# Gated linear attention and channel MLP on one core: keys and queries in three blocks of 384 columns, a new load order at the start, and a re-planned feed-forward

## The chip, the cores and the metric

The kernel runs on one core of one Trainium2 chip. The time is device microseconds of one launch; most executions of one kernel agree within 0.3%. The median of three runs of the kernel before is 1095.43 us (1094.91 to 1096.3).

## The reference

With x of 2048 tokens by 576 channels, all float32:

```python
g = sigmoid((x * gate_w).sum(-1, keepdims=True))
# a: linear attention, 32 heads of 18, phi(t) = where(t > 0, t + 1, exp(t)) + 1e-6
q, k, v = heads(x @ wqkv)                       # wqkv: 576 x 1728
kv, z = einsum("sd,se->de", phi(k), v), phi(k).sum(0)      # per head
o = (phi(q) @ kv) / (phi(q) @ z + 1e-6)
a = o @ wo
# b: mixer channel MLP
h = gelu(layernorm(x) @ w1 + b1)                # w1: 576 x 4608
b = h @ w2 + b2                                 # w2: 4608 x 576
out = g * a + (1 - g) * b
```

## The kernel before

**Precision.** TensorE multiplies in fp32r. Each operand is split into a high part and a low remainder, ScalarE (ACT) rounding the high part and VectorE (DVE) subtracting. A product of a tile of x (576 rows: four chunks of 128 and a tail of 64) with a block of weights is 14 matmuls: `HH`, `HL`, `LH` and two for the tail. `BY_ROWS` and `HI_FIRST` are two orders of those 14.

**Stage 1, keys and queries.** x is cut into 16 tiles of 128 tokens, taken in the order `ORDER`. For each tile `project(i, part, half)` makes the keys and the queries in two halves of 288 columns each, four blocks of 14 matmuls into PSUM banks 6 and 7 in turn. The second half of the keys carries two more columns, the gate's sum and the row sum (290 columns). `phi` then needs two ACT instructions (Relu, Exp) and one DVE instruction a half. `keys_split` splits the keys, and `add_products` (19 matmuls in two parts of 8 and 11) adds the tile's product of keys and x into banks that stay for the whole stage. The queries of a tile go to `acc[i]`.

**The start.** The first three tiles (`FIRST = 3`) are written out by hand. SyncE (SP) issues the loads in the order of the program: x of the first tile, x of the second, the second half of the key weights, x of the third, the first half of the query weights, and so on; ACT's queue loads the first half of the key weights in pieces. The weights are split on ACT and DVE (`split_w`) in the order in which they stand. `first_keys(n, half)` and `first_queries(n, half)` are the 14 matmuls of tile n. The gate's column is transposed in through `turn_gate`.

**The loop** over tiles 3 to 15 (`for n in range(FIRST, NT)`) does per tile: keys half 0, keys half 1, first part of `add_products` of the tile before, queries (both halves), second part. Jobs of the normalized rows (`Y_JOBS`) are hung into numbered slots. The last three tiles (`LATE = 3`) leave their queries for later: one set after the loop, one before the key-value products, one between `transpose_q(0)` and `transpose_q(1)`.

**Stage 2, values.** `project_values(t)` multiplies the masked key-value matrix with the output weights into a pair of banks (`w_pairs`: 6 and 4 in turn), then ACT copies the high part and DVE subtracts the low one into `wp`. `normalize(i, parts)` divides the queries of a tile by their denominators on DVE, and `tail_q(i)` copies the tail on ACT. The order of these calls by hand is the order on each engine.

**Stage 3, attention.** `attend(i)` multiplies 16 tiles of queries with `wp`, 28 matmuls each.

**Stage 4, feed-forward.** Two superblocks of 1024 tokens times 18 chunks of 256 hidden columns. An "up" product (7 a chunk, by a Strassen-like scheme `FACTORS`) is 7 matmuls of 512 columns in two parts of 4 and 3; a "down" unit is 6 (or 12) matmuls of 288 columns. Sums of weights and of hidden parts are put on DVE or on GpSimd (POOL) by the set `ON_DVE`. Chunks in `FIVES` fold their partial sums with copies on ACT in the place of some of the additions on DVE (`make_units`). `plan` simulates all engines with costs (`COST`, and `HEAR`, the time for which a finished instruction is not yet known to the next engine), due times from `TUNED`, and picks the order of all instructions. On TensorE it does a down unit as soon as its slot has come and its inputs are ready within 100 ns, otherwise an up part; `late` says how many parts the ups may run ahead of a down that is not ready. The order that comes out is the order in which each engine runs.

Of the kernel before, what the change touches and what calls it, by code (L numbers as in the profile page):

```python
# [9 lines left out]
F32 = mybir.dt.float32  # L10
F32R = mybir.dt.float32r
AF = mybir.ActivationFunctionType
# [26 lines left out]
LATE = 3  # L39
# [45 lines left out]
DVE_SUMS = set([(2, False), (2, True), (3, True), (4, False), (4, True), (6, False), (6, True)])  # L85
SEEDS = ((0, 0, 0), (0, 1, 1), (1, 0, 1))
Y_EARLY = 5000
ON_DVE = set([('h', 0, 2), ('h', 0, 6), ('h', 1, 3), ('h', 2, 2), ('h', 2, 6), ('h', 3, 4), ('h', 3, 6), ('h', 4, 2), ('h', 5, 3), ('h', 5, 6), ('h', 6, 2), ('h', 6, 3), ('h', 6, 6), ('h', 7, 2), ('h', 7, 6), ('h', 8, 4), ('h', 8, 6), ('h', 9, 4), ('h', 9, 6), ('h', 10, 2), ('h', 10, 4), ('h', 11, 2), ('h', 11, 6), ('h', 12, 4), ('h', 12, 6), ('h', 13, 4), ('h', 14, 4), ('h', 14, 6), ('h', 15, 2), ('h', 15, 4), ('h', 16, 6), ('h', 17, 3), ('h', 17, 4), ('w1', 2, 0), ('w1', 3, 0), ('w1', 10, 0), ('w1', 12, 0), ('w1', 14, 0), ('w1', 16, 0), ('w1', 17, 0), ('w2', 0, 0), ('w2', 4, 0), ('w2', 5, 0), ('w2', 8, 0), ('w2', 10, 0), ('w2', 11, 0), ('w2', 12, 0), ('w2', 14, 0), ('w2', 16, 0)])
FIVES = set([1, 2, 3, 4, 5, 7, 8, 9, 10, 11, 12, 14, 15, 16])
TUNED = (6, 7, 0, 1000, 0, {'unit': -1500, 'ytl': 1500, 'h': -1500, 'yst': 700, 'yhi': -300, 'y': -1500, 'w2': -3000, 'sum': 700, 'p': 700, 'ylo': 300, 'w1sum': -700, 'w1raw': 1500, 'evict': -1500, 'w2hi': -700, 'fin': -700, 'q2': -1500, 'seed': -3000, 'hi': -3000, 'ynorm': 3000, 'forked': -1500, 'ysum': -1500, 'q4': 6000, 'whole': 700, 'u3': -700, 'b2b': -3000, 'q1': 10000, 'out': -300, 'u1': -300, 'end': -700, 'q3': 700, 'w1st': 3000, 'attn': -700, 'fold': -300, 'w2raw': 300, 'yraw': 700}, [2, 5, 250, -500, 600, {'sum': 700, 'u3': 700, 'end': -1500, 'w2sum': -700, 'out': -3000, 'unit': -1500, 'p': -700, 'h': -300, 'evict': -700, 'hi': -1500, 'w1sum': 10000, 'seed': 3000, 'forked': 3000, 'y': 3000, 'q2': -3000, 'u1': -1500, 'q4': 6000, 'w1st': 300, 'ysum': 300, 'w2': 300, 'yraw': 1500, 'whole': 300, 'ynorm': 10000, 'attn': -3000, 'ytl': -1500, 'w1raw': -300, 'q1': 1500, 'yst': 300, 'fin': -300, 'yhi': 700, 'w2raw': 1500, 'w1': 300, 'w2hi': 6000, 'fold': 10000, 'b2b': 700}])  # L90
# [36 lines left out]
def tile_gated_mix(ctx: ExitStack, tc: tile.TileContext, x, xm, xe, wm, we, wvm, wve, wo, um, ue, w2, b1, b2, gw, out):  # L127
# [71 lines left out]
    W, at_ = {}, 0  # L199
    for part in (KEY, QUERY):  # L200
        for half in range(2):
            n = HALF + 2 * (part == KEY and half)
            W[part, half] = ym[:, at_:at_ + 10 * n].rearrange("p (a n) -> p a n", n=n)
            at_ += 10 * n
# [42 lines left out]
    def split_x(i, pieces=((0, 5),)):  # L247
        if i not in xs:
            xs[i] = x_places[PLACE[i] % X_RING]
        to, src = xs[i], xraw[i]  # L250
        for t0, t1 in pieces:
            act.activation(to[:, t0:t1], src[:, t0:t1], AF.Copy)
# [16 lines left out]
    def project(i, part, half, order=BY_ROWS, n=None, between={}):  # L269
        w = W[part, half]  # L270
        p = banks[i, part, half] = ps[:, next(halves_in) if n is None else n]
# [5 lines left out]
    def projected(i, part):  # L277
        for half in range(2):
            project(i, part, half)

    def phi(dst, i, part, half, also=lambda: None):

        p, own = banks[i, part, half][:, :HALF], half_cols(half)
        e = tmp.tile([P, HALF], F32, name="e")
        act.activation(e, p, AF.Relu, scale=-1.0)
        act.activation(e, e, AF.Exp, scale=-1.0)
        also()
        dve.scalar_tensor_tensor(dst[:, own], p, 0.0, e, op0=OP.max, op1=OP.add)
# [3 lines left out]
    def keys_phi(i, half):  # L292
        if half == 0:
            K[i] = kp.tile([P, D], F32, name="k")
        phi(K[i], i, KEY, half, (lambda: None, lambda: sums_of_x(i))[half])

    def sums_of_x(i):
        own = slice(PLACE[i], PLACE[i] + 1)
        act.activation(gsum[:, own], banks[i, KEY, 1][:, HALF:HALF + 1], AF.Copy)
        act.activation(nmean[:, own], banks[i, KEY, 1][:, HALF + 1:HALF + 2], AF.Copy, scale=-1 / D)  # L300
# [21 lines left out]
    def queries_out(i):  # L322
        for half in range(2):
            phi(acc[i], i, QUERY, half)
# [135 lines left out]
    load_x(first[1])  # L460
    load_w(KEY, 1)
    load_x(first[2])
# [10 lines left out]
    split_x(first[0], ((0, 4),))  # L473
# [4 lines left out]
    def first_keys(n, half, between={}):  # L478
        project(first[n], KEY, half, HI_FIRST, 3 * half + n, between)

    def first_queries(n, half):
        project(first[n], QUERY, half, HI_FIRST)

    def both_phi(n):
        for half in range(2):
            keys_phi(first[n], half)
# [32 lines left out]
    phi(acc[first[0]], first[0], QUERY, 0)  # L519
# [4 lines left out]
    phi(acc[first[1]], first[1], QUERY, 0)  # L524
# [3 lines left out]
    phi(acc[first[2]], first[2], QUERY, 0)  # L528
# [6 lines left out]
    phi(acc[first[0]], first[0], QUERY, 1)  # L535
    add_products(first[1], 0)
    phi(acc[first[1]], first[1], QUERY, 1)
# [5 lines left out]
    phi(acc[first[2]], first[2], QUERY, 1)  # L543
# [80 lines left out]
    wo_parts = [ym[:GW, a * G * D:(a + 1) * G * D].rearrange("p (j n) -> p j n", j=G) for a in range(2)]  # L624
    kv_parts = [x_places[PLACE[late[0]] % X_RING - 1][:GW], y_place[:GW, :len(PIECES) * P].rearrange("p (t n) -> p t n", n=P)]
# [21 lines left out]
    projected(late[0], QUERY)  # L647
# [62 lines left out]
    project(late[1], QUERY, 0, n=4)  # L710
    project(late[1], QUERY, 1, n=0)
# [63 lines left out]
    project_values(2)  # L775
    normalize(1, (1,))
    tail_q(1)
    project_values(3)
    project_values(4)
# [3 lines left out]
    for half in range(2):  # L783
        project(late[2], QUERY, half, n=4 + half)
    transpose_q(1)
    tail_q(2)
    queries_out(late[2])
    a1.close()
# [121 lines left out]
    HEAR = {PE: 155, ACT: 33, DVE: 33, POOL: 78, DMA: 30}  # L910
# [140 lines left out]
    def sum_on(what, k, m=0):  # L1051
        own = ((what, k, m) in ON_DVE) != ((m, k < NCHUNK) in DVE_SUMS)
        return (DVE, dve) if own else (POOL, pool)
# [25 lines left out]
    def make_w1(k):  # L1079
# [5 lines left out]
        if k > 1:  # L1085
            dma(lambda: load_w1(k), raw_free["w1"] if k > 2 else [], [("w1raw", k)], 4400, 8, each=560)
            for n in range(4):
                engine, eng = sum_on("w1", k)
# [33 lines left out]
    def make_w2(k):  # L1122
# [4 lines left out]
        if seven:  # L1127
            for n in range(4):
                engine, eng = sum_on("w2", k)
                op(engine, lambda n=n, eng=eng: sum_w2(n, eng), HALF, needs=[("w2raw", k)] + ([("w2sum", k, n - 1)] if n else []),  # L1130
                   gives=[("w2sum", k, n)], port=True)
# [315 lines left out]
    def plan(lag, late, slop, slack, guard, ahead, second=None):  # L1447
        second = second or (lag, late, slop, slack, guard, ahead)
# [23 lines left out]
        next_up, next_down, shift = 0, 0, 0.0  # L1472
# [35 lines left out]
        def choose(e, gently):  # L1508
            if e == PE:
# [4 lines left out]
                if a and b:  # L1514
# [5 lines left out]
                    if ta is not None and tb is not None:  # L1520
                        if tb <= ta + 100:
# [22 lines left out]
        while any(pending.values()):  # L1544
# [6 lines left out]
            e, t = o.engine, s + o.tail  # L1551
            if e == PE:
                shift = s - nominal[o]
                if o.by[0] == "up":
                    next_up += 1
                    if next_up == SECOND:
                        late, slop, slack, guard = second[1:5]
                else:
# [21 lines left out]
            else:  # L1580
                free[e] = s + o.ns
# [62 lines left out]
```

## Time and profile before

| | |
|---|---|
| median of three runs | 1095.43 us |
| the profiled execution | 1096.17 us, its span 1094.5 us |
| TensorE (PE) busy | 1086.3 us, 6712 matmuls |
| DVE, ACT, POOL busy | 922.4, 691.3, 236.2 us |
| granted TensorE clock | 1.00 |
| keys and queries, start to the first kv product | to about 187 us |
| values | 192 to 206 us |
| attention | 206 to 273 us |
| feed-forward | 273 us to the end |

Times of single instructions count from the start of the span. A matmul's row in the profile lasts longer than its turn, since matmuls overlap: a group's pace is read from the start of one group to the start of the next. The name after the engine is the tile written, then those read: `y` holds the weights and x in the first stage and the normalized rows in the feed-forward, `s` is a freshly loaded weight, `t` a freshly loaded x, `region` the split w2, `wa` and `wb` the split w1.

### The profile page before, as it was taken

What the parts mean: (1) busy time and instruction counts of PE and PEld (TensorE: products, weight loads), DVE (VectorE), ACT (ScalarE), POOL (GpSimd) and SP (SyncE); (2) the same over time, 40 slices, a digit from 0 to 9 for tenths busy, and PEclk for the clock granted to TensorE, in tenths of its full rate; (3) what the DMA queues carried; (4) which work ended last, traced back from release to release, by engine and by line L of the source; (5) the groups of instructions that cost most, each with busy time, mean ns of one, the idle gap of its engine ahead of it and who ended that gap; (6) DMA issues with size and microseconds to landing.
All of it is one profiled execution on the core that took longest, in us unless ns stands there. A gap on an engine that the chain in (4) does not pass through costs nothing.

```text
span 1094.5 us, 18650 instructions
## 1 busy us (share of the span) xinstructions
PE 1086.3 (99%) x6712; PEld 996.6 (91%) x6712; DVE 922.4 (84%) x1558; ACT 691.3 (63%) x1235; POOL 236.2 (22%) x232
## 2 busy tenths in 40 slices
PE   9999999999999999999999999999999999999998
PEld 8999999999898889988889988989899999999898
DVE  4568786896799999899999997988887888878888
ACT  6677766454667887777877876455555555455552
POOL 2111113431123232332111202121122211221110
PEclk9999999999999999999999999999999999999999
DMA  6466772745745665764556559574444445444432
GB/s 179 135 87 190 172 218 101 278 178 191 249 156 188 196 203 185 239 209 169 194 184 220 191 197 396 170 252 118 135 148 118 130 119 148 131 122 118 133 102 87
DMA packets 109006, 189.72 MB, mean 173 GB/s; under 512 B 8940, under 2 KB 68604, under 8 KB 104818
## 3 DMA queue, kind: packets, MB, share of 16 engines
q1 hardware_dynamic: 108002, 187.78, 53.7%
q8 instruction: 53, 0.87, 0.3%
q10 hardware_dynamic: 720, 0.74, 0.2%
q14 instruction: 39, 0.32, 0.1%
q0 software_dynamic: 192, 0.01, 0.0%
HBM read 121.70 MB, written 66.80 MB: 172 GB/s over the span
## 4 chain that ended last, share of the span: by engine, by line
PE 92%; DVE 3%; DMA 3%; ACT 1%; issue 0%; SPq 0%; ACTq 0%; DVEq 0%
PE ps L120 92%; DVE accs L120 1%; DMA accs<-moments 1%; DMA yd<-ystage 1%; DMA s<-in_wm 0%; DVE h L120 0%; DMA ystage<-late_acc 0%; DMA fresh<-in_ue 0%; DMA s<-in_we 0%; DVE wa L120 0%; DVE region L120 0%; DVE ystage L120 0%; DVE wb L120 0%; DVE fresh L120 0%; ACT u L120 0%
## 5 line engine op out<-in xcount | busy, mean ns | idle before, releaser
L120 PEld LDWEIGHTS ps<-region,h 128*128 128x128 f32 x3072 | 437.5, 188 | 30.2 <-ACT ps L120 4.7
L120 PE MATMUL ps<-region,h 128*128 128x288 f32 x3072 | 456.8, 295 | 0.8 <-DVE accs L120 0.7
L120 DVE TENSOR_TENSOR accs<-ps,accs 128x576 f32<-128x576 f32 x330 | 246.1, 753 | 60.7 <-PE ps L120 53.9
L120 PE MATMUL ps<-y,wa 128*128 128x512 f32 x1008 | 257.6, 392 | 0.0
L120 PEld LDWEIGHTS ps<-y,wa 128*128 128x128 f32 x1008 | 180.8, 188 | 30.5 <-ACT ps L120 0.2
L120 POOL TENSOR_TENSOR fresh<-fresh 128x288 f32<-128x288 f32 (+1 forms) x128 | 117.1, 918 | 409.5 <-DVE accs L120 144.5
L120 PE MATMUL ps<-y,wb 128*128 128x512 f32 x756 | 199.2, 393 | 0.4 <-ACT u L120 0.4
L120 DVE TENSOR_TENSOR h<-u,h 128x512 fp32r<-128x512 f32 x240 | 165.4, 702 | 8.7 <-ACT u L120 8.7
L120 PEld LDWEIGHTS ps<-y,wb 128*128 128x128 f32 x756 | 133.8, 188 | 21.1 <-ACT u L120 0.6
L120 PE MATMUL ps<-y 128*128 128x288 f32 (+2 forms) x950 | 133.9, 297 | 2.2 <-DVE wp L120 1.1
L120 PEld LDWEIGHTS ps<-y 128*128 128x128 f32 (+1 forms) x950 | 129.8, 188 | 4.4 <-DVE wp L120 1.8
L120 ACT ACTIVATE region<-fresh 128x576 fp32r<-128x576 f32 (+1 forms) x132 | 81.2, 625 | 73.9 <-PE ps L120 73.3
L120 ACT ACTIVATE ps<-ps 128x576 f32<-128x576 f32 (+1 forms) x127 | 78.6, 621 | 45.0 <-PE ps L120 21.5
L120 POOL TENSOR_TENSOR u<-u 128x512 f32<-128x512 f32 x44 | 57.1, 1298 | 193.2 <-DVE h L120 54.8
L120 DVE TENSOR_TENSOR region<-fresh,region 128x576 fp32r<-128x576 f32 (+1 forms) x132 | 94.3, 727 | 1.1 <-ACT region L120 1.1
L120 ACT ACTIVATE u<-ps 128x512 f32<-128x512 f32 x73 | 43.0, 589 | 68.2 <-PE ps L120 68.2
L120 ACT ACTIVATE h<-u 128x512 fp32r<-128x512 f32 x128 | 73.4, 621 | 9.9 <-DVE u L120 5.5
L120 ACT ACTIVATE h<-u,b1s 128x512 fp32r<-128x512 f32 x73 | 52.6, 722 | 42.2 <-DVE u L120 42.1
L120 PE MATMUL ps<-wp,qt 128*128 128x288 f32 x448 | 63.0, 297 | 0.0
L120 DVE TENSOR_TENSOR u<-ps,u 128x512 f32<-128x512 f32 x74 | 50.4, 683 | 13.6 <-PE ps L120 12.7
L120 PEld LDWEIGHTS ps<-wp,qt 128*128 128x128 f32 x448 | 59.8, 188 | 0.0
L120 DVE TENSOR_TENSOR u<-u 128x512 f32<-128x512 f32 x84 | 58.0, 691 | 1.7 <-POOL u L120 1.1
(139 smaller groups left out, 1044.8 us busy)
## 6 DMA issues: line engine op xcount, KB each, us to landing
w1d<-wa SPq DMA_DIRECT2D x17, 1280.0 KB
wa<-w1d SPq DMA_DIRECT2D x68, 320.0 KB
fresh<-in_w SPq DMA_DIRECT2D x70, 288.0 KB
y<-yd SPq DMA_DIRECT2D x14, 1280.0 KB
w1d<-wb SPq DMA_DIRECT2D x17, 960.0 KB
wb<-w1d SPq DMA_DIRECT2D x51, 320.0 KB
yd<-ystage SPq DMA_DIRECT2D x28, 320.0 KB
fresh<-in_um SPq DMA_DIRECT2D x64, 128.0 KB
```

The costliest lines, as they stand in the source:

```text
L120: self.last = self.tc.keep_in_program_order(op(*args, **kwargs))
```

## The change

Three things are edited.

1. **Blocks of 384.** From the fourth tile on, the keys and queries of a tile are three blocks instead of four halves: block 0 is keys 0 to 383; block 1 is keys 384 to 575, the two sum columns and queries 0 to 191 (386 columns); block 2 is queries 192 to 575. The split weights lie in one array so that the blocks are slices of it; the first three tiles still use the halves. `LATE` becomes 4, and only block 2 is left for later. The places of two later operands (`wo_parts`, `kv_parts`) follow the new layout.
2. **The start and the hand-written order.** The third x is loaded ahead of the second half of the key weights, and split and multiplied with the first half before that second half is split. The high part of the first x is copied on DVE and not on ACT. The first half of the query weights is split ahead of `both_phi(0)`. In stage 2 `project_values(3)` moves ahead of `normalize(1, (1,))`, and `tail_q(1)` behind `project_values(4)`.
3. **The feed-forward's plan.** `HEAR` becomes 65 ns for ACT and DVE (33 before), 110 for POOL (78), 300 for DMA (30). TensorE's runs are costed by the place of a matmul in its run (`EACH`). The sets `ON_DVE` (each sum for itself) and `FIVES` (13 chunks, 14 before: 3 and 16 leave, 17 comes) and the numbers of `TUNED` are new; a rule `hold` and `wait` is added.

```diff
-LATE = 3
+LATE = 4
+BLOCK = 384
+REST = D - BLOCK
...
-FIVES = set([1, 2, 3, 4, 5, 7, 8, 9, 10, 11, 12, 14, 15, 16])
-TUNED = (6, 7, 0, 1000, 0, {...}, [2, 5, 250, -500, 600, {...}])
+HEAR_NS = {"PE": 155, "ACT": 65, "DVE": 65, "POOL": 110, "DMA": 300}
+FIVES = set([1, 2, 4, 5, 7, 8, 9, 10, 11, 12, 14, 15, 17])
+TUNED = (6, 12, 0, 0, -500, {...}, [2, 5, 250, -1000, 2000, {...}, 21, 0], 7, 0)
...
+    at_ = 10 * (2 * D + 2)
+    weights = ym[:, :at_].rearrange("p (a n) -> p a n", a=10)
+    FIRST_Q = D + 2
+    W = {(KEY, 0): (0, HALF), (KEY, 1): (HALF, FIRST_Q), (QUERY, 0): (FIRST_Q, FIRST_Q + HALF), (QUERY, 1): (FIRST_Q + HALF, FIRST_Q + D),
+         0: (0, BLOCK), 1: (BLOCK, FIRST_Q + REST), 2: (FIRST_Q + REST, FIRST_Q + D)}
...
+    def keys_phi(i, n):
+        if n in (0, (KEY, 0)):
+            K[i] = kp.tile([P, D], F32, name="k")
+        if n == 0:
+            phi(i, n, [(K[i][:, :BLOCK], 0)])
+        elif n == 1:
+            phi(i, n, [(K[i][:, BLOCK:], 0), (acc[i][:, :REST], REST + 2)], lambda: sums_of_x(i, n, REST))
+        else:
+            phi(i, n, [(K[i][:, half_cols(n[1])], 0)], lambda: sums_of_x(i, n, HALF) if n[1] else None)
...
     load_x(first[1])
+    load_x(first[2])
     load_w(KEY, 1)
-    load_x(first[2])
...
-    split_x(first[0], ((0, 4),))
+    split_x(first[0], ((0, 4),), on_dve=True)
...
     first_keys(1, 0)
+    split_x(first[2])
+    first_keys(2, 0)
     dve.tensor_copy(wraw[KEY, 1][:, :, HALF:HALF + 1], column[:, :, None])
     dve.memset(wraw[KEY, 1][:, :, HALF + 1:HALF + 2], 1.0)
     split_w(KEY, 1)
-    split_x(first[2])
     load_x(ORDER[3])
     first_keys(0, 1)
     first_keys(1, 1)
+    split_w(QUERY, 0)
     both_phi(0)
-    split_w(QUERY, 0)
-    first_keys(2, 0)
     first_keys(2, 1)
...
-        project(i, KEY, 0)
+        project(i, 0)
         keys_phi(i, 0)
-        project(i, KEY, 1)
+        project(i, 1)
...
         if n < NT - LATE:
-            projected(i, QUERY)
+            project(i, 2)
             queries_out(i)
...
     project_values(2)
+    project_values(3)
     normalize(1, (1,))
+    project_values(4)
     tail_q(1)
-    project_values(3)
-    project_values(4)
     normalize(2, (0,))
     transpose_q(0)
     normalize(2, (1,))
-    for half in range(2):
-        project(late[2], QUERY, half, n=4 + half)
+    for n in range(2):
+        project(late[2 + n], 2, at_=4 + n)
...
-    HEAR = {PE: 155, ACT: 33, DVE: 33, POOL: 78, DMA: 30}
+    HEAR = HEAR_NS
+    EACH = {"up": (226.8, (6.3, 9.3, -2.7, 4.3, 9.3, 1.5, 5.5, 4.2)), "down": (131.9, (0, 3, -1, -2, 7, 1, 2, 3, -6, 1, 0, 1))}
...
-                        if tb <= ta + 100:
+                        if tb <= ta + 100 and not (run[0] == "up" and run[1] < hold and behind < wait and ta <= free[PE]):
                             ta = None
```

More of the change, by code (lines that the diff above doesn't have):

```diff
@@ L198, in tile_gated_mix @@
     TERMS = ((0, 0), (0, 1), (1, 0))
-    W, at_ = {}, 0
-    for part in (KEY, QUERY):
-        for half in range(2):
-            n = HALF + 2 * (part == KEY and half)
-            W[part, half] = ym[:, at_:at_ + 10 * n].rearrange("p (a n) -> p a n", n=n)
-            at_ += 10 * n
+    at_ = 10 * (2 * D + 2)
[3 more added lines that the diff above has]
+         0: (0, BLOCK), 1: (BLOCK, FIRST_Q + REST), 2: (FIRST_Q + REST, FIRST_Q + D)}
+    W = {key: weights[:, :, c0:c1] for key, (c0, c1) in W.items()}
     y_place = ym[:, at_ + X_RING * 9 * P:][:, :2 * 5 * P]
@@ L267, in tile_gated_mix, with project @@
     halves_in, banks = cycle((6, 7)), {}
-    def project(i, part, half, order=BY_ROWS, n=None, between={}):
-        w = W[part, half]
-        p = banks[i, part, half] = ps[:, next(halves_in) if n is None else n]
+    def project(i, n, order=BY_ROWS, at_=None, between={}):
+        w = W[n]
+        p = banks[i, n] = ps[:, next(halves_in) if at_ is None else at_]
         for m, (a, b) in enumerate(order):
@@ L322, in queries_out, with half_queries_out @@
     def queries_out(i):
-        for half in range(2):
-            phi(acc[i], i, QUERY, half)
+        phi(i, 2, [(acc[i][:, REST:], 0)])
+    def half_queries_out(i, half):
+        phi(i, (QUERY, half), [(acc[i][:, half_cols(half)], 0)])
     KC = 448
@@ L518, in tile_gated_mix @@
     both_phi(2)
-    phi(acc[first[0]], first[0], QUERY, 0)
+    half_queries_out(first[0], 0)
     split_xn(first[0])
@@ L523, in tile_gated_mix @@
     first_queries(2, 0)
-    phi(acc[first[1]], first[1], QUERY, 0)
+    half_queries_out(first[1], 0)
     for part in range(2):
@@ L527, in tile_gated_mix @@
     split_w(QUERY, 1)
-    phi(acc[first[2]], first[2], QUERY, 0)
+    half_queries_out(first[2], 0)
     first_queries(0, 1)
@@ L542, in tile_gated_mix @@
     add_products(first[1], 1)
-    phi(acc[first[2]], first[2], QUERY, 1)
+    half_queries_out(first[2], 1)
     keys_split(first[2])
@@ L646, in tile_gated_mix @@
     split_wo(2, 4)
-    projected(late[0], QUERY)
+    project(late[0], 2)
     queries_out(late[0])
@@ L787, in tile_gated_mix @@
     queries_out(late[2])
+    queries_out(late[3])
     a1.close()
@@ L1445, in tile_gated_mix, with plan @@
     assert len(in_order) == len(ops)
-    def plan(lag, late, slop, slack, guard, ahead, second=None):
-        second = second or (lag, late, slop, slack, guard, ahead)
+    def plan(lag, late, slop, slack, guard, ahead, second, hold, wait):
         slot, due = {o: n for n, o in enumerate(ups)}, {}
@@ L1471, in plan, with streams @@
         port_at, moved, landed = {e: 0 for e in port_until}, 0.0, []
-        next_up, next_down, shift = 0, 0, 0.0
+        next_up, next_down, shift, run = 0, 0, 0.0, ["", 0]
+        def streams(o):
+            n = round(o.ns / (231.7 if o.by[0] == "up" else 132.3))
+            each, more = EACH[o.by[0]]
+            at_ = run[1] if run[0] == o.by[0] else 0
+            return n, n * each + sum(more[at_:at_ + n])
         def offer(o):
@@ L1550, in plan @@
             s, _, o = min(picks, key=lambda x: x[:2])
-            e, t = o.engine, s + o.tail
+            e, t, ns = o.engine, s + o.tail, o.ns
             if e == PE:
+                n, ns = streams(o)
+                t += ns - o.ns
+                run[:] = o.by[0], n + (run[1] if run[0] == o.by[0] else 0)
                 shift = s - nominal[o]
@@ L1557, in plan @@
                         late, slop, slack, guard = second[1:5]
+                        hold, wait = second[6:8]
                 else:
```

63 lines of the change are left out of this document (30 added, 33 removed).

## The prediction

> **What bounds the kernel now.** I read the page first, then the list of waits of TensorE, then busy time by stage, then the timeline where something waits.
>
> ```profile
> span 1094.5 us, 18650 instructions
> PE 1086.3 (99%) x6712; PEld 996.6 (91%) x6712; DVE 922.4 (84%) x1558; ACT 691.3 (63%) x1235; POOL 236.2 (22%) x232
> PE 92%; DVE 3%; DMA 3%; ACT 1%; issue 0%; SPq 0%; ACTq 0%; DVEq 0%
> ```
>
> The second line is the busy time of each engine, the third the chain of work that ended last. TensorE (PE) is the bound. Its waits, and the stages (columns: stretch, its length, busy time and count of PE, weight loads, DVE, ACT, POOL, granted clock, DMA share, GB/s):
>
> ```profile
> PE ps L120 <- DVE wp L120: 1.1, 1, 1.1
> ...
> PE ps L120 <- DVE accs L120: 0.7, 1, 0.7
> PE ps L120 <- ACT u L120: 0.4, 1, 0.4
> ```
>
> ```profile
> 14.48:192.00 177.52, 177.52 (x1194) 170.06 (x1194) 124.65 (x267) 125.21 (x280) 32.45 (x25) 1.00 0.56 148
> 273.10:700.00 426.90, 426.40 (x2502) 381.79 (x2501) 398.27 (x657) 319.45 (x528) 103.21 (x98) 1.00 0.61 209
> 700.00:1090.50 390.50, 389.81 (x2338) 353.90 (x2336) 329.82 (x498) 202.87 (x334) 72.33 (x76) 1.00 0.45 134
> ```
>
> The reader should see that PE is full for the whole key and query stage, at clock 1.00, and that there are few waits to take away. So the time can fall in two ways only: fewer or shorter matmuls, or those few waits. Every part is costed as PE time.
>
> **Part 1, blocks of 384.** Per tile 56 matmuls of 288 (half of the keys 290) become 42 of 384 to 386; the columns stay the same, so what is saved is the part of a matmul that doesn't depend on its columns. One period of the loop, PE alone:
>
> ```profile
> 78.64 3.88 PE L120 MATMUL ps<-y 128*128 128x288 f32 x28
> ...
> 84.34 3.90 PE L120 MATMUL ps<-y 128*128 128x288 f32 x28
> 88.08 0.85 PE L120 MATMUL ps<-xs,ks 128*128 128x512 f32 x3
> 88.77 1.23 PE L120 MATMUL ps<-ks,xs 128*128 128x512 f32 x5
> 89.84 3.88 PE L120 MATMUL ps<-y 128*128 128x288 f32 x28
> ```
>
> Start to start, 28 matmuls of 288 take 88.08 - 84.34 = 3.74 us, 133.6 ns each; three of 512 take 88.77 - 88.08 = 0.69 us, 230 ns each. A line through both is 0.430 ns a column and 9.7 ns fixed; at 384 it gives 174.9 ns. A tile then takes 42 x 174.9 = 7.35 us in the place of 7.48, a gain of 0.13 us. The 0.69 is rounded; with 0.68 (227 ns) the line gives 173.6 ns and 0.19 us. I take 0.15 us, 13 tiles: **-2.0 us** (1.7 to 2.5). It doesn't matter where in the stage a block runs, since PE is full there, so `LATE = 4` costs nothing as long as no bank is waited for: blocks alternate between two banks and each has 14 matmuls of another block, some 2.4 us, to be emptied by two ACT instructions and one DVE pass, which is longer than now (1.87 us). ACT issues six instructions of `phi` a tile and not eight; DVE keeps four. ACT has 125 of 178 us, so this moves nothing.
>
> [...]
>
> **Part 2, the start.** The second half of the key weights is waited for:
>
> ```profile
> 4.69 0.74 SPq L120 DMA_DIRECT2D s<-in_wm  x1
> ...
> 7.90 0.58 SPq L120 DMA_DIRECT2D t<-in_xm  x1
> ...
> 8.56 3.45 PE L120 MATMUL ps<-y 128*128 128x288 f32 x24
> ...
> 11.30 1.42 ACT L120 ACTIVATE y<-s 128x1450 fp32r<-128x1450 f32 x1 [2.43 <-DMA s<-in_we]
> ...
> 12.75 1.67 DVE L120 TENSOR_TENSOR y<-s,y 128x1450 fp32r<-128x1450 f32 x1 [2.80 <-ACT y L120]
> 12.77 1.48 PE L120 MATMUL ps<-y 128*128 128x290 f32 x9 [0.76 <-ACT y L120]
> ...
> 14.48 12.14 PE L120 MATMUL ps<-y 128*128 128x290 f32 x89 [0.23 <-DVE y L120]
> ```
>
> ```profile
> 4.70:11.20 6.50, 6.50 (x44) 6.14 (x44) 3.77 (x10) 3.15 (x7) 0.00 (x0) 1.00 0.90 250
> ```
>
> PE ends the first-half products of two tiles at 8.56 + 24 x 0.134 = 11.77. It starts on the second half at 12.77, does the nine matmuls that need only high weights by 13.97, and waits for DVE's low part until 14.48: 1.0 + 0.5 us lost. After the change 14 more matmuls stand in that hole, to 13.64. Their price is on the queue: on SP the third x (two more loads behind it) takes the places from 4.69 on, and the weights move to 7.90. The DMA engines were 0.90 busy at 250 GB/s, so the delay is the bytes of one x, 5 x 128 x 128 x 4 = 328 KB: 1.3 us. The weights land at 12.6, ACT splits to 14.02, PE starts at 14.05, its nine end at 15.25, DVE's low part is there at 15.7, and the 33 left end at 20.15. Before, the same work (47 matmuls after 14.48) ended at 20.78: **-0.6 us**. Bounds: without any delay of the weights all 42 run from 13.64 to 19.27, -1.5; with the full 7.90 - 4.69 = 3.2 us they end at 22.0, +1.3. I take the bytes, since the engines were nearly full.
>
> What else moves here I cost at nothing. The third x is split on ACT and DVE between 9 and 11.3, when ACT waits (the 2.43 in its row). The copy of the first x on DVE takes 128x512 off ACT, but PE's first products wait for pieces of weights that still come when they came. `split_w(QUERY, 0)` now stands on ACT before the first `phi`, which waits for PE anyway; were those weights late, `phi` would queue behind, and with it the banks of the first keys, which `add_products` needs only after the first queries.
>
> **Part 3, the values.** The longest wait of PE (1.1):
>
> ```profile
> 198.68 1.26 DVE L120 SCALAR_TENSOR_TENSOR accs<-accs,den 128x576 f32<-128x576 f32 x1
> ...
> 199.82 0.60 PE L120 MATMUL ps<-accs 128*128 128x128 f32 x4
> 199.98 0.31 ACT L120 ACTIVATE tail<-accs 128x128 f32<-128x128 f32 x1 [2.00 <-DVE accs L120]
> 200.19 1.17 ACT L120 ACTIVATE wp<-ps 128x576 fp32r<-128x576 f32 x2
> ...
> 200.86 1.42 DVE L120 TENSOR_TENSOR wp<-ps,wp 128x576 fp32r<-128x576 f32 x2 [0.92 <-ACT wp L120]
> 201.67 3.99 PE L120 MATMUL ps<-y 128*128 128x288 f32 x28 [1.14 <-DVE wp L120]
> ```
>
> The late queries use the banks of `project_values(3)`. Its ACT copy stands behind `tail_q(1)`, which waits (2.00) for the normalization on DVE (198.68 to 199.94). After the change the copy follows its matmuls, whose last six (of `project_values(4)`) end at 199.8, so it can start by 199.0: ACT to 199.65, DVE to 200.35. PE ends its transposes at 200.5 and goes on. **-1.1 us** (0 to 1.14). Late next: the normalization, now 200.35 to 201.6, then the `wp` of the last piece to 202.3 and tile 2's first part to 203.6; they are needed by the attention, which starts two blocks (4.9 us) later, at 206. `tail_q(1)` has the same room.
>
> **Part 4, the feed-forward.** No matmul is added or removed. What can go is waits and the price of changing between ups (512) and downs (288):
>
> ```profile
> 714.11 0.86 PE L120 MATMUL ps<-y,wb 128*128 128x512 f32 x3
> 715.65 1.59 PE L120 MATMUL ps<-region,h 128*128 128x288 f32 x10 [0.69 <-DVE accs L120]
> ```
>
> ```profile
> 279.51 4.92 PE L120 MATMUL ps<-y,wb 128*128 128x512 f32 x21
> 284.27 6.56 PE L120 MATMUL ps<-y,wa 128*128 128x512 f32 x28
> ...
> 400.69 1.78 PE L120 MATMUL ps<-y,wa 128*128 128x512 f32 x7
> 402.31 1.75 PE L120 MATMUL ps<-region,h 128*128 128x288 f32 x12
> ```
>
> At 714 three ups take 1.54 us where 0.69 is due: 0.85 us lost, more than the 0.69 that the row shows as idle; the other wait is 0.4. In a long run an up takes (284.27 - 279.51)/21 = 226.7 ns, in a run of seven (402.31 - 400.69)/7 = 231.4. The new plan knows this price, but its rule `hold` acts only where `behind < wait`, with `wait` 0, while a down is not considered at all where `behind` is below 0: it is inert, and runs stay near seven. So I take the two waits: **-1.2 us**. Best: those and a quarter of 1764 x 4.7 ns = 8.3 us, -3.3. Worst by DVE, whose work grows in the first superblock:
>
> ```profile
> L120 DVE TENSOR_TENSOR accs<-ps,accs 128x576 f32<-128x576 f32 x330 | 246.1, 753 | 60.7 <-PE ps L120 53.9
> L120 DVE TENSOR_TENSOR u<-u 128x512 f32<-128x512 f32 x84 | 58.0, 691 | 1.7 <-POOL u L120 1.1
> L120 DVE TENSOR_TENSOR fresh<-fresh 128x384 f32<-128x384 f32 x28 | 15.4, 572 | 0.5 <-DMA fresh<-in_ue 0.5
> ```
>
> One chunk of `FIVES` fewer is four more additions of 753 ns; counting the sets, five more sums of 572 ns and two fewer of 691 come to DVE there: 3.0 + 2.9 - 1.4 = +4.5 us, on 398 of 427 busy. It hides in the 29 us left; without that cover it costs up to 4.5.
>
> **The sum.** -2.0 - 0.6 - 1.1 - 1.2 = -4.9 us. Against the profiled execution's 1096.17 that is 1091.3; the median of the runs is 0.7 lower, so **1090.5**.
>
> **The rivals.**
> (a) *The plan changes nothing*: inert rule, other small waits for the old. For it: only two waits to win in 817 us of feed-forward. 1095.4 - 3.7 = 1091.7.
> (b) *A matmul's time is all columns*: 384/288 x 133.6 = 178.1 ns, 42 of them 7.48 us, part 1 gains nothing: 1092.5. Against it: 512 columns by this would take 237.5, and take 230. [...]
> (c) *The feed-forward gives it back*: new waits of 3 to 4 us (DVE is at 93% in the first superblock), total 1094 to 1096. For it: 0.85 us went at a single place in the present order. Within 0.2%.
> (d) *Slower*: DVE becomes the bound of the first superblock. The added 4.5 us land on PE, and each down that waits for its addition also stops the ups behind it; at one wait like 714's (0.85 us) in six of the 18 chunks, 5.1 more: 1095.4 - 3.7 + 9.6 = 1101.3. It decides when more than 3.7 us land on PE, measurably at 5.9. Against it: 29 us of idle DVE.
>
> **How the numbers follow.** 0.2%, 2.2 us, is about what a measurement of this kernel can tell from no change. Forecast 0.56, (a) 0.13, (b) 0.05, (c) 0.18, (d) 0.08. Forecast, (a) and (b) are faster: 0.74; (c) same, 0.18; (d) slower, 0.08. Low end: all best bounds, 1.5 + 2.5 + 1.14 + 3.3 = 8.4, to 1087.0. High end 1094.6, into (c): it leaves out (d) and a good half of (c).
>
> **What would show it.** The loop's period 11.20 (78.64 to 89.84) falls to 11.05; PE has 13 x 14 = 182 fewer matmuls, 6530; the wait for `wp` is gone; the split of the 1450-column weights starts near 12.6 and the first-stage waits there sum to 0.9; the first up starts 3.7 us earlier, at 269.4; DVE's busy time to 700 rises by about 4 us without a wait of PE over 0.5. Wrong if the period stays at 11.2, or the feed-forward from its first up to the end is not between 818 and 822 us (now 821.4).

## The result and the profile after

The changed kernel takes 1101.52 us (median of 5 runs, 1100.64 to 1102.66), the kernel before in the same session 1095.8: a ratio of 1.0057, 95% interval 1.0047 to 1.0068. It is slower by 0.57%, where 0.4% faster was forecast. The profiled execution is the slowest of the five, 1102.66 us. The page of after, the lines that answer to those of before:

```profile
span 1101.0 us, 18199 instructions
PE 1086.8 (99%) x6530; PEld 999.2 (91%) x6530; DVE 932.4 (85%) x1583; ACT 687.8 (62%) x1202; POOL 219.0 (20%) x212
```

PE has the 182 matmuls fewer, and yet is as long busy as before: a row's busy time hides a part of what a matmul waits for (0.16 of the 0.85 us lost at 714.11 in the profile of before) and what a slower clock adds (in a stretch at clock 0.50, below, 3.41 of 3.41 us are busy). What PE waits for (total, times, longest):

```profile
PE ps L122 <- ACT y L122: 5.1, 5, 2.0
PE ps L122 <- DVE accs L122: 2.3, 1, 2.3
PE ps L122 <- DVE y L122: 1.8, 3, 1.1
...
PE ps L122 <- DVE wp L122: 0.2, 1, 0.2
```

The wait for `wp` is down to 0.2, as forecast, and the waits for `y` and `accs` are 9.2 us in the place of 1.7. Four starts on PE cut each span into pieces, those of before first (start, length, work), then those of after:

```profile
39.54 3.63 PE L120 MATMUL ps<-y 128*128 128x288 f32 x26
...
181.44 1.13 PE L120 MATMUL ps<-pks,ones 128*128 128x288 f32 x4
...
273.13 6.54 PE L120 MATMUL ps<-y,wa 128*128 128x512 f32 x28
```

```profile
8.89 5.29 PE L122 MATMUL ps<-y 128*128 128x288 f32 x38
16.18 5.69 PE L122 MATMUL ps<-y 128*128 128x290 f32 x29 [2.00 <-ACT y L122]
22.57 1.33 PE L122 MATMUL ps<-y 128*128 128x290 f32 x8 [0.70 <-ACT y L122]
24.26 4.66 PE L122 MATMUL ps<-y 128*128 128x290 f32 x33 [0.36 <-DVE y L122]
31.20 2.13 PE L122 MATMUL ps<-y 128*128 128x288 f32 x14 [2.28 <-DVE accs L122]
...
46.26 4.01 PE L122 MATMUL ps<-y 128*128 128x384 f32 x22
...
57.36 5.06 PE L122 MATMUL ps<-y 128*128 128x384 f32 x28
62.26 0.86 PE L122 MATMUL ps<-xs,ks 128*128 128x512 f32 x3
...
68.46 5.06 PE L122 MATMUL ps<-y 128*128 128x384 f32 x28
...
177.74 3.22 PE L122 MATMUL ps<-ks,xs 128*128 128x512 f32 x16
181.51 0.44 PE L122 MATMUL ps<-y 128*128 128x384 f32 x1 [0.55 <-ACT y L122]
183.06 0.98 PE L122 MATMUL ps<-y 128*128 128x384 f32 x4 [1.11 <-DVE y L122]
184.32 3.25 PE L122 MATMUL ps<-y 128*128 128x384 f32 x9 [0.29 <-DVE y L122]
187.37 0.93 PE L122 MATMUL ps<-xs,ks 128*128 128x512 f32 x3
...
191.19 1.13 PE L122 MATMUL ps<-pks,ones 128*128 128x288 f32 x4
...
202.53 7.56 PE L122 MATMUL ps<-y 126*128 126x288 f32 x51 [1.40 <-ACT y L122]
...
283.45 6.54 PE L122 MATMUL ps<-y,wa 128*128 128x512 f32 x28
```

| piece | before | after | difference |
|---|---|---|---|
| start to tile 3 | 39.54 | 46.26 | +6.72 |
| tile 3 to the sums of the keys (`pks`) | 141.90 | 144.93 | +3.03 |
| to the first up | 91.69 | 92.26 | +0.57 |
| feed-forward (span 1094.46, 1100.95) | 821.33 | 817.50 | -3.83 |

They add to the 6.5 us between the two spans. Not all of the 6.72 comes each time: two later profiles of kernels with the same start, e2 and e10, reach tile 3 at 43.96 and 43.75. The loop itself is faster: its period is 68.46 - 57.36 = 11.10 in the place of 11.20. The loss lies ahead of it, in the first 46 us, and behind it, in one late block (181.51) and one product of the values (202.53). The busy time by stage (stretch, length, PE, weight loads, DVE, ACT, POOL, granted clock, DMA share, GB/s) shows one more thing:

```profile
283.40:700.00 416.60, 416.60 (x2454) 376.05 (x2453) 393.02 (x659) 310.68 (x512) 93.30 (x90) 1.00 0.61 211
...
16.84:20.25 3.41, 3.41 (x17) 3.37 (x16) 0.98 (x1) 0.00 (x0) 0.00 (x0) 0.50 1.03 286
184.09:187.50 3.41, 3.17 (x10) 3.18 (x11) 0.18 (x1) 0.00 (x0) 0.00 (x0) 0.50 0.00 0
```

The clock was 1.00 in the first stage of before; here two stretches of 3.41 us ran at 0.50, each just behind a wait. And in the first superblock PE now waits for nothing (416.60 of 416.60).

**The theory.** The blocks of 384 overlap the halves, so all weights of keys and queries now lie in one array, ten rows (five chunks, high and low) of 1154 columns, and a half or a block is a strided slice of all rows. The waits look as if such a slice were taken for everything from its first to its last element. Then the split of the second half of the keys would wait for products that only read the first half; the products of that half, when they reach the second row, for the split of the queries, which stands behind it in the program; the late block for `split_wo`, which writes other columns of the same rows; and `project_values` for the copy into the last rows of `kv_parts`, between whose first and last element lie rows of the other operand, `wo_parts`. In the kernel before each half had a piece of memory of its own. The places of the waits fit to the matmul: of the products with the second half of the keys 29 go ahead, two tiles and the first of the third, which reads the first row, where these columns end ahead of the queries' (22.57); eight more go until the one that reads the last low row (24.26); and in the values three go ahead of the first that reads a row of `wo_parts` between those of the copy (202.53). The rivals were the load order, the half clock, and the new plan.

### The profile page after: what moved, and what is told of

It is laid out like the page before. It is cut to its first block, busy times and chain, and to the rows that moved or that the text cites. A ratio compares the mean times of both kernels' runs of the same rounds, so it can differ in the third digit from the quotient of the medians.

```text
span 1101.0 us, 18199 instructions
## 1 busy us (share of the span) xinstructions
PE 1086.8 (99%) x6530; PEld 999.2 (91%) x6530; DVE 932.4 (85%) x1583; ACT 687.8 (62%) x1202; POOL 219.0 (20%) x212
## 4 chain that ended last, share of the span: by engine, by line
PE 95%; DMA 1%; DVE 1%; ACT 1%; SPq 0%; issue 0%; ACTq 0%; DVEq 0%
PE ps L122 95%; DMA s<-in_wm 1%; DVE y L122 0%; ACT e L122 0%; SPq L122 0%; DMA t<-in_xe 0%; DVE ks L122 0%; ACT y L122 0%; DVE den L122 0%; DVE accs L122 0%; ACT ks L122 0%; DVE kvs L122 0%; ACTq L122 0%; DVE k L122 0%; DVE xs L122 0%
## 5 line engine op out<-in xcount | busy, mean ns | idle before, releaser
L122 PE MATMUL ps<-region,h 128*128 128x288 f32 x3072 | 452.2, 295 | 0.0
L122 POOL TENSOR_TENSOR fresh<-fresh 128x288 f32<-128x288 f32 (+1 forms) x98 | 85.7, 877 | 394.2 <-DVE h L122 172.5
L122 PE MATMUL ps<-y 128*128 128x384 f32 (+4 forms) x768 | 136.6, 332 | 9.3 <-ACT y L122 5.1
L122 POOL TENSOR_TENSOR u<-u 128x512 f32<-128x512 f32 x54 | 71.9, 1331 | 221.4 <-DVE h L122 139.8
L122 DVE TENSOR_TENSOR region<-fresh,region 128x576 fp32r<-128x576 f32 (+1 forms) x132 | 89.0, 692 | 2.1 <-ACT region L122 2.0
L122 ACT ACTIVATE u<-u,b1s 128x512 f32<-128x512 f32 x73 | 52.5, 721 | 1.5
```

The costliest lines, as they stand in the source:

```text
L122: self.last = self.tc.keep_in_program_order(op(*args, **kwargs))
```

## The experiments

Each is compared with runs of the kernel before on the same chip, whose median was 1095.3, 1095.26 or 1095.1.

**The plan alone** (e1_plan_only): the kernel before with part 3 of the change, and nothing of parts 1 and 2.

```diff
-    HEAR = {PE: 155, ACT: 33, DVE: 33, POOL: 78, DMA: 30}
+    HEAR = HEAR_NS
... (ON_DVE, FIVES, TUNED, EACH, hold and wait as in the change)
```

> The kernel before with part 3 alone (the new plan of the feed-forward). Theory: the loss lies ahead of the feed-forward, whose own stretch fell from 821.3 to 817.5 us in the two traces; alone it gives 1095.8 - 3.8 = 1092.0 us. Rival (d) of the prediction, the plan is what costs because DVE becomes the bound: 1098 us or more.

Measured: 1091.82, ratio 0.997 (0.996 to 0.9981). The plan is worth 3.5 us whatever stands ahead of it, and isn't what makes the change slower. Its feed-forward by stage, beside that of the kernel before:

```profile
273.30:1087.00 813.70, 813.70 (x4837) 736.61 (x4836) 737.07 (x1178) 523.27 (x856) 158.93 (x154) 1.00 0.54 175
```

```profile
273.10:1090.50 817.40, 816.22 (x4838) 735.68 (x4836) 728.09 (x1154) 522.32 (x862) 175.54 (x174) 1.00 0.53 173
```

Rival (d)'s 1098 falls. DVE has 9 us more work, and PE's idle time goes from 1.18 us to nothing; the other 2.5 us of these 3.7 are in gaps too short for the list of waits (below).

**The late part row by row** (e2_late_rows): the change, with `split_wo` cut so that one instruction touches one row, and `kv_parts[0]` in a place of its own.

```diff
-    split_wo(0, 2)
-    split_wo(2, 4)
+    for j in range(4):
+        split_wo(j, j + 1)
-    kv_parts = [weights[:GW, :len(PIECES), FIRST_Q:FIRST_Q + P], ...]
+    kv_parts = [x_places[PLACE[late[0]] % X_RING][:GW], ...]
```

> The changed kernel, with the four output-weight splits done row by row, so that each writes one unbroken stretch of the weight array, and with the first key-value operand moved from columns of that array to a free x place. Theory (a strided access counts as everything between its first and its last element, so products wait for splits of other columns): the waits of 0.55, 1.11 and 0.29 us before the late block and of 1.40 us in the values go, and with them the half clock at 184 us (about 1.5 us); 4.1 + 1.4 = 5.5 us, so 1096.0 us. Rival (the products need what they wait for, or ACT and DVE are simply late): same or slower by the extra instructions, 1101 to 1102 us.

Measured: 1096.38, ratio 1.0012 (1.0002 to 1.0021), 5.1 us less than the change, near the 1096.0 of the theory. The start is untouched: five of the eleven runs, with a mean clock of 0.999 or 1.000, took 1094.9 to 1095.7, six with 0.998 took 1096.4 to 1097.7. The same bytes are copied, and PE's late block and the product of the values run in one piece:

```profile
178.50 2.60 PE L122 MATMUL ps<-y 128*128 128x384 f32 x14
180.94 0.86 PE L122 MATMUL ps<-xs,ks 128*128 128x512 f32 x3
...
194.25 8.24 PE L122 MATMUL ps<-y 126*128 126x288 f32 x54
```

The late block takes 180.94 - 178.50 = 2.44 us; in the change it ended 4.1 us late (the 16 products ahead of it begin at 177.74 and take 3.06 us in e2; 177.74 + 3.06 + 2.44 = 183.24, against 187.37).

**The start row by row** (e3_start_rows): the change, with three splits of weights cut into their rows.

```diff
-    split_w(KEY, 1)
+    split_w(KEY, 1, pieces=((0, 1), (1, 2), (2, 3), (3, 4), (4, 5)))
... (the same for QUERY 0 and QUERY 1)
```

> The changed kernel, with the splits of the second half of the key weights and of both halves of the query weights done row by row. Theory (strided extents): the key weights still land at 14.5 us, but PE no longer waits for the query splits at 22.6, 24.3 and 31.2 us (0.7, 1.0 and 2.3 us), and starts on the keys after the first row and not after all five, about 1 us earlier: 1101.5 - 4.5 = 1097.0 us; the half clock after the wait for the loads stays. Rival (the start's loss is the load order alone): 1101 to 1102 us, since the loads are as they were.

Measured: 1096.95, ratio 1.0018 (1.0009 to 1.0028), 4.6 us less than the change, as the theory had it.

```profile
8.30 14.92 PE L122 MATMUL ps<-y 128*128 128x288 f32 x108
24.55 2.13 PE L122 MATMUL ps<-y 128*128 128x288 f32 x14 [1.33 <-DVE accs L122]
...
39.60 1.56 PE L122 MATMUL ps<-y 128*128 128x384 f32 x8
...
174.86 0.44 PE L122 MATMUL ps<-y 128*128 128x384 f32 x1 [0.55 <-ACT y L122]
176.40 4.29 PE L122 MATMUL ps<-y 128*128 128x384 f32 x13 [1.11 <-DVE y L122]
```

108 products of three tiles in one unbroken run where the change had four pieces: the three waits for `y` are gone, and those of the late block, left as they were, are there to the hundredth. Ten instructions on single rows copy the same values as two on five rows; so at 22.57 and 24.26 it was neither the data nor the engine that PE waited for. The first of the three waits (16.18) is another matter: those products need the split. Here its first row was split at 11.58, when the main part of the weights had landed, while the whole in one copy began at 14.71 in after, behind the last of the loads.

**The loads in their old order** (e4_loads_back): the change, with the third x loaded behind the second half of the key weights.

```diff
+    load_w(KEY, 1)
     load_x(first[2])
-    load_w(KEY, 1)
```

> The changed kernel with one line moved: the third x is loaded behind the second key weights again, as before. Theory (strided extents): the key weights land at 11.2 us again, but their split must wait for the products of the third x, which now lands at 12.1 us; PE waits about as long as in the changed kernel, only elsewhere: 1101 to 1102.5 us. Rival (the load order alone is the loss of the start): the keys start 3.3 us earlier, and without the half clock 1.7 more: 1096.5 to 1098 us.

Measured: 1103.02, ratio 1.007 (1.0057 to 1.0082), 0.5 above the theory's range; the rival's 1096.5 to 1098 falls. Two rows of ACT in it, the splits of the second half of the keys and of the first half of the queries, name what holds them; the row of PE has a wait that after has too (31.20), but here the 14 products behind it take 33.75 - 30.33 = 3.42 us, in after 33.17 - 31.20 = 1.97. The mean clock of this profile is 0.997, as in after:

```profile
14.87 1.41 ACT L122 ACTIVATE y<-s 128x1450 fp32r<-128x1450 f32 x1 [1.79 <-PE ps L122]
20.22 1.41 ACT L122 ACTIVATE y<-s 128x1440 fp32r<-128x1440 f32 x1 [3.93 <-PE ps L122]
...
30.33 3.63 PE L122 MATMUL ps<-y 128*128 128x288 f32 x14 [2.30 <-DVE accs L122]
```

A copy of freshly loaded weights waits for PE, whose products read other columns. The same copy of the 1450 columns waited for a DMA before (11.30). In e2, which has the loads of the change, it waits for PE as well (1.81 us, at 13.45); in the profile of after the DMA came last (14.71).

**The load order alone** (e5_load_order_only): the kernel before, with only the load of the third x moved ahead.

```diff
+    load_x(first[2])
     load_w(KEY, 1)
-    load_x(first[2])
```

> The kernel before with one line moved: the third x is loaded ahead of the second key weights, all else (halves in separate arrays, order of products and splits, plan) as before. In the changed kernels those weights landed between 12.1 and 14.5 us, against 11.2 before. Here nothing stands in the hole, so each us of delay is one us of PE: 1095.3 + 0.9 to 3.3, with the half clock up to 1.7 more: 1096.5 us. Rival (the forecast's price, the bytes of one x, 1.3 us): 1096.6 us, the same here; a result at 1095.3 would mean that the load order costs nothing.

Measured: 1098.08, ratio 1.0026 (1.0017 to 1.0035), which is 2.8 us and more than the 1.2 of the sum. In its profile:

```profile
14.28 1.48 PE L120 MATMUL ps<-y 128*128 128x290 f32 x9 [1.60 <-ACT y L120]
```

PE starts 14.28 - 12.77 = 1.5 us later, close to the 1.3 forecast from the bytes. Of the ten runs the four with a mean clock of 1.00 took 1096.5 to 1097.5, the six with 0.996 to 0.998 took 1098.1 to 1100.3: the rest goes with the half clock. The one trace is of a run at 1.00, so that the half clock stands behind this wait, now 1.6 us long, is not shown.

**Products of ones ahead of the late block** (e10_warm_late): the change, with 14 products of `ones` in the bank of the late block before it, so that PE doesn't idle there.

```diff
-    project(late[0], 2)
+    bank_late = next(halves_in)
+    for _ in range(14):
+        pe.matmul(ps[:, bank_late, :P], ones, ones, start=True, stop=True)
+    project(late[0], 2, at_=bank_late)
```

> The changed kernel with 14 matmuls of ones (3.0 us, into a bank that the next product overwrites) ahead of the late block, where TensorE waits from 181 to 184 us. Theory (the wait also halves the clock for 3.4 us): the wait stays, the clock stays at 1.00, and the block after it runs at 174 ns a matmul and not 340: the work done at 187.4 is done at 186.5, so 1100.5 us. Rival (the slow block after the wait has another cause): 1101.5 us or more, half clock or not.

Measured: 1100.15, ratio 1.0047 (1.0034 to 1.006), 1.4 us less than the change. The block then runs at full pace, at a clock of 1.00 from 178.29 to 187.60, and takes 183.86 - 181.33 = 2.53 us against 187.37 - 181.51 = 5.86:

```profile
178.29 3.29 PE L122 MATMUL ps<-ones 128*128 128x128 f32 x28
181.33 2.69 PE L122 MATMUL ps<-y 128*128 128x384 f32 x14
183.86 0.86 PE L122 MATMUL ps<-xs,ks 128*128 128x512 f32 x3
```

From tile 3 to the products behind the block it is 183.86 - 43.75 = 140.11 us in the place of 187.37 - 46.26 = 141.11. So 1.0 of the 1.4 us is the half clock behind the waits of this block, near the forecast; the other 0.4 isn't from this edit as far as the rows show, since three of the five runs, the profiled one among them, have a mean clock of 1.000 and so no half clock at the start either (an estimate: 3.41 of 1100 us at 0.50 would make the mean 0.998). The waits themselves this kernel sits out in its products of ones (181.33 - 178.29 = 3.04 us).

**Both repairs** (e9_rows_all): the change with the edits of e2 and e3 together.

```diff
+    for j in range(4):
+        split_wo(j, j + 1)
+    kv_parts = [x_places[PLACE[late[0]] % X_RING][:GW], ...]
+    split_w(KEY, 1, pieces=((0, 1), (1, 2), (2, 3), (3, 4), (4, 5)))
... (the same for QUERY 0 and QUERY 1)
```

> The changed kernel, its own start kept, with both fixes: all later splits into the weight array row by row, the key-value operand in a free x place. Theory: with its start done row by row the fourth tile begins at 39.6 us, as before (39.5), so 1090.2 us; the third x ahead of the key weights is worth nothing. If the two fixes merely add up, 1101.5 - 5.1 - 4.5 = 1091.9 us. Rival (the new load order costs by itself): 1091.5 us or more, over 1 us above the same kernel with the old start.

Measured: 1091.81, ratio 0.9974 (0.9963 to 0.9985). That is 9.7 us less than the change, the sum of 5.1 and 4.6, but 1.6 more than I expected and where the rival has it. One long wait is left:

```profile
25.79 2.13 PE L122 MATMUL ps<-y 128*128 128x288 f32 x14 [2.28 <-DVE accs L122]
```

**Both repairs and the start of before** (e6_both_fixed): the same, with the loads, the order of the calls and the copy of the first x as in the kernel before.

```diff
+    load_w(KEY, 1)
     load_x(first[2])
-    load_w(KEY, 1)
...
     first_keys(1, 0)
-    split_x(first[2])
-    first_keys(2, 0)
...
-    split_w(QUERY, 0, ...)
     both_phi(0)
+    split_w(QUERY, 0, ...)
+    first_keys(2, 0)
```

> Blocks of 384, the new values order and the new plan, with the start of the kernel before (its loads, its order of products and splits, the first x on ACT), and with all later splits into the weight array row by row and the key-value operand in a free x place. Theory (strided extents cost the front 10 us, everything else is as forecast): the plan alone gave 1091.8; from the fourth tile to the first up the row-wise late kernel takes 231.9 us against 233.6 before, so 1091.8 - 1.7 = 1090.1 us. Rival (blocks of 384 gain nothing, only the plan does): 1091.8 us or more.

Measured: 1089.29, ratio 0.9947 (0.9934 to 0.9961), faster than both kernels and 0.8 below the 1090.1 expected; the rival's 1091.8 falls. PE's waits in all, and the start:

```profile
PE ps L122 <- DVE ones L122: 1.1, 1, 1.1
PE ps L122 <- ACT y L122: 0.7, 2, 0.5
PE ps L122 <- DVE wp L122: 0.2, 1, 0.2
```

```profile
8.69 16.65 PE L122 MATMUL ps<-y 128*128 128x288 f32 x122
...
38.27 5.07 PE L122 MATMUL ps<-y 128*128 128x384 f32 x28
...
179.00 1.13 PE L122 MATMUL ps<-pks,ones 128*128 128x288 f32 x4
...
269.84 6.54 PE L122 MATMUL ps<-y,wa 128*128 128x512 f32 x28
```

**The order of one split** (e11_phi_first): e9 with `split_w(QUERY, 0)` back behind `both_phi(0)`, to tell which part of the new start costs the 2.5 us between e9 and e6.

```diff
-    split_w(QUERY, 0, ...)
     both_phi(0)
+    split_w(QUERY, 0, ...)
```

> The run before with both repairs and the change's own start (e9) took 1091.8 and its one real wait of PE was 2.28 us, for the bank that the queries of the first tile leave; here only the split of the first half of the query weights goes back behind `both_phi(0)`, the load order stays the new one. Theory, that this wait is the queue behind that split: the wait is gone or under 0.5, tile 3 starts 1.5 to 2.5 us earlier than 40.84, the time is 1089.3 to 1090.3. Rival, that the new load order itself costs the 2.5 us against the version with the old start (1089.3): the time stays within 0.7 of 1091.8 and PE waits elsewhere in the first 40 us.

Measured: 1091.75, ratio 0.9969 (0.9958 to 0.9979). My theory fell: the wait went only from 2.28 to 1.71. In the two profiled executions (1091.77 and 1091.27) tile 3 starts 0.54 earlier, at 40.30 and not 40.84; the medians, 0.06 apart with runs that spread by 1.8 us and more, can't resolve that. The time is where the rival has it, but its cause, the load order, is not shown by that: e6 has the old order of products too, and no run has the one without the other. The row of ACT is the first pass over the second half of the first tile's keys, the rows of DVE and PE are the pass that empties the bank and the products that wait for it, in e11 and then in e6; the last row is ACT's split of the first half of the query weights in e9:

```profile
16.11 0.41 ACT L122 ACTIVATE e<-ps 128x288 f32<-128x288 f32 x1 [0.89 <-PE ps L122]
...
24.74 0.46 DVE L122 SCALAR_TENSOR_TENSOR accs<-ps,e 128x288 f32<-128x288 f32 x1 [0.65 <-ACT e L122]
...
25.25 2.12 PE L122 MATMUL ps<-y 128*128 128x288 f32 x14 [1.71 <-DVE accs L122]
```

```profile
14.07 0.41 ACT L122 ACTIVATE e<-ps 128x288 f32<-128x288 f32 x1 [0.41 <-PE ps L122]
...
22.70 0.46 DVE L122 SCALAR_TENSOR_TENSOR accs<-ps,e 128x288 f32<-128x288 f32 x1 [0.65 <-ACT e L122]
```

```profile
15.85 1.78 ACT L122 ACTIVATE y<-s 128x288 fp32r<-128x288 f32 x5 [1.43 <-DMA s<-in_wm]
```

From ACT's pass to the one that frees the bank lie 8.63 us in both runs (24.74 - 16.11, 22.70 - 14.07), and both times ACT had waited for PE, which works without a gap. In e11 the 14 products of the third x stand ahead of the first tile's second half, at 0.136 us each (122 take 16.65 us in e6) 1.9 us. ACT's pass comes 2.04 us later than in e6, the bank 2.04, tile 3 2.03 (40.30, 38.27). PE's own products ahead of that bank end at 8.69 + 108 x 0.136 = 23.4 in e6, when the bank is free. So the products that fill the hole put off what ACT and DVE need next, and their queue, not PE, sets the end of the start.

In e9 the queue is held elsewhere: the split of the query weights stands ahead of the pass, and ACT waits 1.43 us for these weights to land. From there to the bank are 25.28 - 15.85 = 9.43 us, and in e3, with the same start, 24.04 - 14.62 = 9.42. The split of the key weights, which begins 2.2 us later than in e6 (12.65 in e11, 10.47 in e6, both when their main part had landed), is in none of these chains.

## Why the prediction was wrong

**Where it went.** Of the 6.3 us between the change and the 1095.26 of before, the repairs of the layout take away 9.7, half clocks behind the waits included (the change against e9, of two sessions; 9.1 by the two ratios), the new start costs 2.5 (e9 against e6), and what is left of the change, with the splits by rows, gains 6.0 (e6 against before). By the rows of e6 that gain is 1.3 at the start (tile 3 at 38.27, before at 39.54), 1.2 from there to the sums of the keys, and the rest in the values and the feed-forward. The 1.3 aren't the change's own: by rows the split of the key weights begins when their main part has landed (10.47), as a whole only with the last load (11.30), and PE needn't wait for a whole half to be split. The 9.7 hold such a gain of the finer split too; no run separates it.

**The step that failed** is in part 1: "It doesn't matter where in the stage a block runs, since PE is full there, so `LATE = 4` costs nothing as long as no bank is waited for". I costed the matmuls, and not the move that makes the blocks possible, the weights in one array. Banks were the only shared thing that I asked about. In the sum the move stands at nothing; its repairs were worth 9.7 us. That the waits come from the layout is shown: e2 and e3 change only how many rows one copy touches and where one operand lies, and take the waits away each at its place. That a slice is taken from its first to its last element is the reading that fits all of them, to the matmul; it was not tried by itself.

**Part 1, the blocks.** 28 matmuls of 384 take 62.26 - 57.36 = 4.90 us, 175.0 ns each, where the line gave 174.9. The period fell by 0.10 and not 0.15, so 1.3 us and not 2.0, under the bound of 1.7: the rows of the products between the blocks, 11.10 - 42 x 0.175 = 3.75 us, were 3.72 before. From tile 3 to the sums of the keys e6 takes 140.73 against 141.90 of before, 1.2 less. Rival (b), no gain, is wrong.

**Part 2, the start.** Without the layout's waits the new start is 2.5 us slower than the old one (e9 against e6), where -0.6 was forecast, with bounds of -1.5 to +1.3. Its delay of 1.3 was near: in e5, where the loads alone were changed, the split begins at 12.82, 1.5 us later than before (11.30, both behind the last load), and 12.6 was forecast; in the profile of after it began only at 14.71. And PE did fill the hole, as forecast: e9 has no gap from 8.80 to 23.51. What failed is "What else moves here I cost at nothing": I took PE as the bound behind the hole, and counted the products that fill it as won. The bound is the queue of ACT and DVE, which begins with the first tile's keys, and those 14 products put the keys off by 2.0 us (e11). The call that I named as a danger, `split_w(QUERY, 0)`, was one: in e9 these weights are late, ACT waits 1.43 us for them and `phi` behind it, and the wait for the bank is 0.6 longer (2.28 against 1.71). The waits at the start, which were to sum to 0.9, are 2.00 + 0.70 + 0.36 + 2.28 = 5.3 us in after.

**Part 3, the values.** The wait for `wp` is 0.18 in the place of 1.14, as said (-1.0 against -1.1). The 1.40 us at 202.53 that replaced it are the layout's, and are gone in e2.

**Part 4, the plan.** -3.5 (e1) to -3.8 (after), where -1.2 was taken and -3.3 was the best bound. The mechanism, waits that go, was right and the size was not: I priced the two waits of the list. Counted from the start of each matmul to the next, the feed-forward of before has 28 gaps over 60 ns beyond their due, 3.9 us in all, and after has 2, 0.2 us; 25 of the 28 are of 0.06 to 0.11 us, which no wait in the list shows. The runs of ups hardly grew (298 before, 279 after, on average 5.9 and 6.3 matmuls), as forecast. DVE's share of the first superblock rose from 398.27/426.90 = 93.3% to 393.02/416.60 = 94.3%, 4.5 us on the old length (+4.5 forecast), and it hid. So rival (d), which ends at 1101.3, has the number of the result and none of its mechanism.

**The other signs.** 6530 matmuls: right. First up at 269.4: 283.45 in after, 269.84 in e6, which is the change without the two things that I hadn't costed, the layout and the queue behind the new start. The feed-forward's 817.5 is outside 818 to 822, on the good side.

## What to carry to other kernels

When operands that had memory of their own become slices of one array, ask of every copy into it which earlier reads and later writes now overlap from first to last element; a copy cut into rows and a second place kept them apart here, and were worth 9.7 us. A hole on the busiest engine is only worth filling if what fills it doesn't put off what the other engines wait for (the new start, which does, was 2.5 us slower, e9 against e6): follow their queue from the product that comes later to the buffer that is needed next. And small gaps count, 25 of 0.06 to 0.11 us in the feed-forward of before: price a stream of matmuls from start to start, not from the list of its waits.

## What the runs showed of the hardware

A wait of about 2 us was followed by a slower clock in some places, and so cost more than itself. In after, TensorE's clock was 0.50 for 3.41 us (16.84 to 20.25) behind 2.00 us of waiting (16.18), and for 3.41 us again (184.09 to 187.50) behind 0.55 and 1.11 (181.51, 183.06); nine products of 384 took 187.37 - 184.32 = 3.05 us there, 339 ns each, where 28 in the loop took 175.0 each (57.36). In e3 it was 0.50 from 176.88 to 180.30, behind the same 0.55 and 1.11 (174.86, 176.40). In the 3.41 us ahead of each of these three stretches PE idled 2.00, 1.70 and 1.66 us.

It didn't come each time. The 2.28 us ahead of 31.20 in after were followed by a clock of 1.00, and the 14 products behind them took 1.97 us; in e9 the same wait of 2.28 was followed by 27.76 - 25.79 = 1.97 us for them, in e4 2.30 were followed by 3.42. In the profile of after the two stretches begin 167.25 us apart, 49 times the 3.413 us that each lasted by the trace's record of the clock. Cut into pieces of that length from the end of the first stretch on (20.25), the 2.28 us lie in two pieces, of which PE idled 1.57 (27.08 to 30.49) and 0.71 us (30.49 to 33.90). Ahead of 0.50 it was 1.66 or more; whether that is what decides, no run tried.

The landing of one and the same load moved by more than a microsecond between profiles: with the third x ahead of them and a split by rows, the key weights' split began at 11.58 (e3), 12.63 (e9) and 12.65 (e11), waiting for the DMA of their main part in each. SP issued that load at 6.98 in e3 and at 8.21 in after, with the same order of loads, so a difference of this size was there at the issue.
